# Fetching the second half's first operands one block later, and another order of statistics and copies in the opening

## The chip, the cores and the metric

The kernel runs on one core of a Trainium2 chip. The metric is device time in microseconds (us), the median of three runs. The core has five engines with instruction queues of their own, each worked through in order: TensorE (PE; its weight loads are shown as PEld), VectorE (DVE), ScalarE (ACT), GpSimd (POOL) and SyncE (SP). SP computes nothing here. It issues nearly all DMA transfers, and a transfer that has to wait for something holds up all transfers behind it in SP's queue. Tiles lie in SBUF, matmul results in PSUM banks.

## The reference

All values are float32. x has 2048 rows of 1024 features, there are 32 heads of 32 features, and the hidden width of the gated part is 3584.

```python
xn = layernorm(x)
# A: linear attention with learned softmax features
q, k, v = split(xn @ wqkv)                     # 32 heads of 32
pq, pk = q @ w_phi, k @ w_phi                  # per head
phi_q = concat(softmax(pq), softmax(-pq))
phi_k = concat(softmax(pk), softmax(-pk))
num = phi_q @ (phi_k^T @ v)
den = phi_q @ sum_s(phi_k) + 1e-6
s = (num / den) @ wo
# B: gated feed-forward
out = (silu(xn @ w1) * (xn @ w3)) @ w2
result = x + s * silu(out)
```

## The kernel before

Every float32 operand is split in two parts, a high one (a cast to a 32-bit matmul type, on ACT) and the low rest (a subtraction, on DVE). `split` (L92) does both, so L95 is the cast and L96 the subtraction. A product takes three passes (`PASSES`, L90). The large products are multiplied two by two in blocks with seven products instead of eight. The seven are listed in `ORDER`: each names a PSUM bank (a, b or c) and its two operands, A11, A12, S2, S1, S3, S4, A22 from the rows and B11, B21, T2, T1, T3, B22, T4 from the weights.

The first large stage is gate and up (x @ w1, x @ w3). It goes over the rows in two halves, tb 0 and 1. In each half it goes over 28 feature blocks f, and in each block over the seven products j. One such product is a step: 12 matmuls of 128x512 on TensorE (L655). The list `events` holds all steps in order. `gate_up(step)` issues a step's matmuls and whatever else is tied to it, and returns `read`, which reads the bank: copies and activations on ACT, additions and products on DVE.

The instructions of this stage are recorded in the order in which the code writes them (`in_order`, engine by engine). No scheduler moves them. What is tied to which step is set by tables:

- `load_at`: when the weights of a later block are fetched (`b_load`, `b_part`, L265, two transfers of 512 KB into one of two buffers named rw).
- `sums_at`: when the sums of the weight blocks are made (`b_sums`, L131 and L132).
- `prep_at`: when the next of the seven weight operands is split (`b_operands`).
- `before` and `after`: side work that rides along, such as `side_kv` (prepares the weights for the keys and values from tiles of the pool "xp", and stores the splits as wkv_d, L454) and `side_fold`.

`gate_up` also fetches the row operands of the second half. The operands of the first half lie in seven large slots. Two more slots belong to the pool "spare", which is opened only when the pools "xp" and "bdp" are closed, and lies in their place. A transfer into "spare" therefore waits until the last reader of "xp" is done. The first two operands of the second half (A11 and A12, named op1A, four transfers each, `fetch`, L167) go there. The other five follow from the last block on, each when a slot comes free. In the last block of the second half the same lines fetch weights for the next stage.

```python
if f == NF - 3 and j == 0:
    if tb == 0:
        close("xp", "bdp")
        spare = pool("spare", 1, side="right")
    for m in range(2):
        early.update(fetch(tb + 1, m))
```

Ahead of step 4 stands the opening, written out by hand. It loads eight tiles of 128 rows. The first four are normalised and turned (transposed on TensorE, L223), and steps 0 to 3 are computed from them. The other four (late_x) follow: `stats` (mean and variance, L196 and L197), `rstd` (the root on ACT, L203, then a refinement on DVE, L207 to L212), `norm` (L218), the turns, copies out of PSUM (`raw_x`, L228), sums and splits. Between them stand the folds: 12 blocks of the key weights are multiplied with w_phi on TensorE (`first_folds`, L252), copied back by ACT and stored (`first_copies`, L343 and L344), and the next ones are loaded (`load_folds`, L245). Turns and folds share three PSUM banks. `next(gens[0, f])` splits the next weight operand of block f; those in question are the two T2 operands, which step 4 and step 5 need.

Of the kernel before, what the change touches and what calls it, by code (L numbers as in the profile page):

```python
# [20 lines left out]
NF = FF // P  # L21
# [8 lines left out]
def tile_kernel(ctx: ExitStack, tc: tile.TileContext, x, wkT, wqT, wv, wphi, wo, w1, w3, w2, out):  # L30
# [3 lines left out]
    def pool(name, bufs, **kw):  # L34

        open_pools[name] = tc.tile_pool(name=name, bufs=bufs, reuse_waits="tile", **kw)
        return open_pools[name].__enter__()

    def close(*names):
        for name in names:  # L40
            open_pools.pop(name).__exit__(None, None, None)
# [51 lines left out]
    def split(hi, lo, src, by=None):  # L93

        nc.scalar.copy(hi, src)  # L95
        (by or nc.vector).tensor_sub(lo, src, hi.bitcast(F))  # L96
# [58 lines left out]
    def slot(m, j):  # L155
        name = f"op{m}" + (ANAMES if m < 2 else BNAMES)[j]
        j = HOMES[m][j]
        if j < 7:
            return big.tile([P, 2, 4, 512], R, name=name, tag=f"big{j}")
        return spare.tile([P, 2, 4, 512], R, name=name, tag=f"spare{j}")  # L160

    def fetch(m, j):
        t = slot(m, j)
        if m < 2:
            n = ANAMES[j]
            for q in range(4):
                nc.sync.dma_start(t[:, :, :, q * P:(q + 1) * P].bitcast(F), xo_d[m][n][:, q])  # L167
        else:
            n = BNAMES[j]
            nc.sync.dma_start(t.bitcast(F), wkv_d[(1, 2, 0)[m - 2]][n])  # L170
        return {n: t}
# [7 lines left out]
    def flat(t):  # L179
        return t.rearrange("p k t -> p (k t)")  # L180
# [12 lines left out]
    def stats(mv, j, xt):  # L193
        st = small.tile([P, 2, 6], F, name="st")
        for a in range(2):
            nc.vector.bn_stats(st[:, a, :], xt[a])  # L196
        nc.vector.bn_aggr(mv[:, j], st.rearrange("p a b -> p (a b)"))  # L197
# [50 lines left out]
    def fold(wr, c):  # L248

        pw = ps.tile([P, 4, P], F, name="pw", tag="tr", bufs=3)  # L250
        for g in range(4):
            nc.tensor.matmul(pw[:, g, :], wr[:, g], bd[:, 4 * c + g, :], start=True, stop=True)  # L252
        return pw
# [3 lines left out]
    def b_load(f):  # L257

        rw = rwp.tile([P, 2, 2, 512], F, name="rw", tag="rw")
        for a in range(2):  # L260
            b_part(rw, f, a)
        return [rw[:, a, h] for a in range(2) for h in range(2)]
# [25 lines left out]
    ao, xs = {n: slot(0, j) for j, n in enumerate(ANAMES) if n in ("A11", "A12", "S2", "S1")}, []  # L288
# [38 lines left out]
    def first_split(n, qs=range(4)):  # L327
        for q in qs:
            sl = slice(q * P, (q + 1) * P)
            split(ao[n][:, 0, :, sl], ao[n][:, 1, :, sl], raw[q][n])  # L330

    def first_folds(n):
        for _ in range(n):
            k = first_folds.at
            assert k not in to_load
            to_copy.append((k, fold(fold_rooms[k % 6], folds[k][2])))
            first_folds.at += 1

    def first_copies(n):
        for _ in range(n):  # L340
            k, pw = to_copy.pop(0)
            wr = fold_rooms[k % 6]
            nc.scalar.copy(wr, pw)  # L343
            nc.sync.dma_start(folds[k][3], flat(wr))  # L344
# [23 lines left out]
    mvs = [consts[:, 8 + 8 * k:16 + 8 * k].rearrange("p (j a) -> p j a", a=2) for k in range(2)]  # L368
# [15 lines left out]
    def blk2(k):  # L384
        if not rooms:
            rooms.extend(big.tile([P, 8, 512], F, name="room", tag=f"big{j}") for j in (2, 3))
        return rooms[k // 8][:, k % 8]
# [214 lines left out]
    for u in range(2 * NKB):  # L602
        f = 4 * (u // 2) + 2 * (u % 2)
# [20 lines left out]
    xo, early, gens, bos, silus = {}, {}, {}, {}, []  # L624
# [3 lines left out]
    def gate_up(step):  # L628
        nonlocal spare
        tb, f, j = events[step]  # L630
        last = f == NF - 1
        b, an, bn = ORDER[j]
        if f == NF - 3 and j == 0:
            if tb == 0:
                close("xp", "bdp")
                spare = pool("spare", 1, side="right")
            for m in range(2):
                early.update(fetch(tb + 1, m))
        for late in load_at.get(step, ()):
            rws.append(b_load(late[1]))  # L640
        for do in before.pop(step, ()):
            do()
        bank = banks.setdefault((tb, f), {})

        paired = (tb, f) == (1, 1)
        first = b not in bank
        if first:
            if paired and b == "a":
                bank[b] = ps.tile([P, 512], F, name="banka", tag="tr", bufs=3)
            else:  # L650
                bank[b] = ps.tile([P, 512], F, name=f"bank{b}", bufs=BANKS[b])
        n = 0
        for k in range(4):
            for u, w in PASSES:
                nc.tensor.matmul(bank[b], bos[tb, f][bn][:, w, k], ao[an][:, u, k], start=first and n == 0,  # L655
                                 stop=LAST[b] == an and n == 11, skip_group_check=True)
                n += 1
        for g in prep_at.get(step, ()):
            next(gens[g])
        for g in sums_at.get(step, ()):  # L660
            bos[g] = {}
            gens[g] = b_operands(rws.pop(0), bos[g])
            next(gens[g])
        for do in after.pop(step, ()):
            do()

        def read():

            nonlocal ao, early, hs, even, even_d, bank
            def part(name):  # L670
                if paired:
                    t = blk2(10 + len(part_names))
                    part_names.append(name)
                else:
                    t = flat(blk(name)) if (tb, f) == (0, 1) else work.tile([P, 512], F, name=name, tag="w")
                parts[tb, f, name] = t
                return t

            h0, u0, u1 = (parts.get((tb, f, name)) for name in ("h0", "u0", "u1"))
            hd = h_d[tb][f // 4][:, :, :, f % 2, f % 4 // 2]  # L680
            if an == "A11":
                nc.scalar.copy(part("h0"), bank["b"])
            elif an == "A12":
                nc.vector.tensor_add(h0, bank["a"], h0)
                if step < 4:
                    silus.append(h0)
                else:
                    nc.scalar.activation(h0, h0, AF.Silu)
            elif an == "S2":
                nc.scalar.copy(part("u0"), bank["b"])  # L690

                for d, b, t in hs:
                    store_h(d, b, t)
                hs = []
            elif an == "S1":
                nc.scalar.copy(part("u1"), bank["c"])
            elif an == "S3":
                nc.vector.tensor_add(u1, bank["b"], u1)  # L698
            elif an == "S4":
                nc.vector.tensor_add(u0, bank["c"], u0)  # L700
                nc.vector.tensor_mul(h0, h0, u0)
                hs.append((hd, 0, h0))
            else:
                h1 = work.tile([P, 512], F, name="h1", bufs=2)
                nc.scalar.activation(h1, bank["b"], AF.Silu)
                nc.vector.tensor_mul(h1, h1, u1)
                if f % 2 == 0:
                    even, even_d = h1, hd
                else:
                    nc.vector.tensor_add(even, even, h1)  # L710
                    hs += [(even_d, 1, even), (hd, 1, h1)]
                for name in ("h0", "u0", "u1"):
                    del parts[tb, f, name]
                del banks[tb, f], bos[tb, f], bank
                h0 = u0 = u1 = h1 = None
            if last and tb:
                xo.update(reload(0, [ANAMES[0], ANAMES[1]] if j == 0 else ANAMES[j + 1:j + 2]))
            if last and j < 5:
                early.update(fetch(tb + 1, j + 2))
            if last and j == 6:  # L720
                ao, early = early, {}

        return read
# [20 lines left out]
    def early_raw(t, h):  # L744
        raw[t][early_at(t, h)[0]] = raw_x(pts.pop((t, h)))
# [25 lines left out]
    reads[0]()  # L771
    for t in range(4):
        early_raw(t, 1)
    next(gens[0, 1])
    reads[1]()
    reads.append(gate_up(2))
    first_folds(2)
    first_copies(2)
    stats(mvs[1], 0, xs[4])
    stats(mvs[1], 1, xs[5])  # L780
    reads[2]()
    reads.append(gate_up(3))
    first_folds(4)
    load_folds(2)
    first_copies(2)

    nc.gpsimd.tensor_copy(consts[:, 1:2], mvs[1][:, 0, 0:1])
    for do in held:
# [3 lines left out]
        stats(mvs[1], t, xs[4 + t])  # L792
    r1 = rstd(mvs[1], sds[1])
    next(r1)
    first_copies(2)
    load_folds(2)
    sd = next(r1)
    for t in range(4):
# [11 lines left out]
    first_sums("S1", (2, 3))  # L810
    first_sums("S2", (2, 3))
    first_split("S2", (2, 3))
    first_folds(2)
    first_copies(2)
    for f in range(2):
        next(gens[0, f])
    first_folds(1)
    first_copies(2)
    assert first_folds.at == FOLDS and not to_copy
# [706 lines left out]
```

## Time and profile before

| what | value |
|---|---|
| runs (us) | 2388.48, 2393.23, 2399.55; median 2393.23 |
| profiled execution, its own time | 2389.33 us |
| its span, first to last instruction | 2387.5 us |
| TensorE busy | 2347.3 us, 98% |
| VectorE busy | 1774.7 us, 74% |
| ScalarE busy | 898.5 us, 38% |
| GpSimd busy | 257.4 us, 11% |
| mean granted TensorE clock | 0.995 |

A row of a timeline reads: start (us from the span's start), length in us, engine, line, operation, output<-input, shape, count, and in brackets the idle time before it with what ended it. Rows of one kind that follow one another on an engine are merged, so the length can span several. SPq is SP's queue issuing a transfer. A row of a waits view reads: engine, what it was about to do, what it waited for, total us, number of times, longest. A row of a windows view gives a stretch, its length, and then the busy time (with the count of instructions) of PE, PEld, DVE, ACT and POOL, the granted clock, the DMA share and the GB/s.

### The profile page before, as it was taken

What the parts mean: (1) busy time and instruction counts of PE and PEld (TensorE: products, weight loads), DVE (VectorE), ACT (ScalarE), POOL (GpSimd) and SP (SyncE); (2) the same over time, 40 slices, a digit from 0 to 9 for tenths busy, and PEclk for the clock granted to TensorE, in tenths of its full rate; (3) what the DMA queues carried; (4) which work ended last, traced back from release to release, by engine and by line L of the source; (5) the groups of instructions that cost most, each with busy time, mean ns of one, the idle gap of its engine ahead of it and who ended that gap; (6) DMA issues with size and microseconds to landing.
All of it is one profiled execution on the core that took longest, in us unless ns stands there. A gap on an engine that the chain in (4) does not pass through costs nothing.

```text
span 2387.5 us, 37640 instructions
## 1 busy us (share of the span) xinstructions
PE 2347.3 (98%) x14592; PEld 1924.1 (81%) x14592; DVE 1774.7 (74%) x2777; ACT 898.5 (38%) x1577; POOL 257.4 (11%) x243
## 2 busy tenths in 40 slices
PE   7999999997999999999999999999999999999999
PEld 6888888886888888888788888887888888888787
DVE  7877778884688888875466665777577888786775
ACT  5545444443355544543212221334433333353000
POOL 1000000000000000000000000331012222213562
PEclk9999999998999999999999999999999999999999
DMA  5446689995988898954977878997435653479763
GB/s 214 146 163 216 225 280 309 322 306 191 310 289 277 301 301 286 302 200 169 400 285 258 318 256 292 366 332 256 154 126 158 203 177 132 150 246 274 206 185 103
DMA packets 298354, 578.03 MB, mean 242 GB/s; under 512 B 24624, under 2 KB 151744, under 8 KB 295488
## 3 DMA queue, kind: packets, MB, share of 16 engines
q1 hardware_dynamic: 291840, 552.56, 68.8%
q10 hardware_dynamic: 6336, 23.07, 2.4%
q8 instruction: 115, 1.88, 0.3%
q14 instruction: 63, 0.52, 0.1%
HBM read 372.64 MB, written 202.91 MB: 241 GB/s over the span
## 4 chain that ended last, share of the span: by engine, by line
PE 94%; DVE 2%; DMA 2%; SPq 1%; ACT 0%; issue 0%; POOL 0%; DVEq 0%; ACTq 0%; POOLq 0%
PE bankb L655 25%; PE bankb L1280 13%; PE bankc L655 12%; PE pm L1432 8%; PE bankb L875 7%; PE bankc L1280 6%; PE banka L655 6%; PE bankb L942 4%; PE bankc L875 3%; PE banka L1280 3%; PE bankc L942 2%; PE banka L875 2%; PE po L1417 1%; PE banka L942 1%; PE pkv L860 1%; DMA op2T<-wkv_d1T 1%
## 5 line engine op out<-in xcount | busy, mean ns | idle before, releaser
L96 DVE TENSOR_TENSOR bo<-rw,bo 128x512 fp32r<-128x512 f32 x336 | 230.8, 688 | 153.6 <-ACT bo L95 153.2
L1280 PE MATMUL bankb<-bo,as 128*128 128x512 f32 x960 | 235.2, 389 | 1.3 <-ACT acc L1286 1.3
L95 ACT CAST bo<-rw 128x512 fp32r<-128x512 f32 x336 | 206.7, 618 | 17.6 <-DMA w_d2B<-w2o 3.1
L1280 PEld LDWEIGHTS bankb<-bo,as 128*128 128x128 f32 x960 | 180.1, 188 | 39.1 <-ACT acc L1286 1.7
L655 PE MATMUL bankb<-op0S,bo 128*128 128x512 f32 x672 | 166.5, 398 | 14.8 <-ACT u L690 14.0
L655 PE MATMUL bankc<-op0S,bo 128*128 128x512 f32 x672 | 163.6, 392 | 0.3 <-DVE op0S L96 0.3
L655 PEld LDWEIGHTS bankb<-op0S,bo 128*128 128x128 f32 x672 | 128.4, 192 | 42.8 <-ACT u L690 14.4
L655 PE MATMUL bankb<-op1S,bo 128*128 128x512 f32 x672 | 161.2, 389 | 0.0
L655 PE MATMUL bankc<-op1S,bo 128*128 128x512 f32 x672 | 161.2, 389 | 0.0
L1432 PE MATMUL pm<-wos,oT 128*128 128x512 f32 x672 | 160.0, 393 | 0.0
L655 PE MATMUL bankb<-op0A,bo 128*128 128x512 f32 x672 | 159.2, 391 | 0.7 <-ACT op0A L738 0.7
L852 POOL MEMSET ev<- 128x32 f32 x32 | 4.2, 132 | 1435.6 <-DVE bo L96 1100.0
L1280 PE MATMUL bankc<-bo,as 128*128 128x512 f32 x624 | 158.4, 389 | 0.0
L655 PE MATMUL bankb<-op1A,bo 128*128 128x512 f32 x672 | 157.6, 390 | 0.0
L655 PEld LDWEIGHTS bankc<-op0S,bo 128*128 128x128 f32 x672 | 125.4, 188 | 30.1 <-issue 2.9
L655 PEld LDWEIGHTS bankb<-op1A,bo 128*128 128x128 f32 x672 | 125.9, 188 | 27.4 <-DVE u L698 1.3
L655 PEld LDWEIGHTS bankb<-op0A,bo 128*128 128x128 f32 x672 | 125.2, 188 | 27.9 <-ACT op0A L738 0.9
L655 PEld LDWEIGHTS bankc<-op1S,bo 128*128 128x128 f32 x672 | 126.1, 188 | 26.2
L655 PEld LDWEIGHTS bankb<-op1S,bo 128*128 128x128 f32 x672 | 126.1, 188 | 26.2
L1432 PEld LDWEIGHTS pm<-wos,oT 128*128 128x128 f32 x672 | 124.8, 188 | 27.5 <-DVE oT L1423 0.3
L1280 PEld LDWEIGHTS bankc<-bo,as 128*128 128x128 f32 x624 | 117.1, 188 | 24.4
L1294 DVE TENSOR_TENSOR acc<-bankb,acc 128x512 f32<-128x512 f32 x152 | 102.0, 685 | 31.2 <-PE bankb L1280 31.2
(272 smaller groups left out, 4332.4 us busy)
## 6 DMA issues: line engine op xcount, KB each, us to landing
rw<-in_w SPq DMA_DIRECT2D x112, 512.0 KB, 4.5
hr<-h_d SPq DMA_DIRECT2D x56, 512.0 KB, 4.7
h_d<-h SPq DMA_DIRECT2D x111, 256.0 KB, 5.2
xoS<-xo_d0S SPq DMA_DIRECT2D x44, 512.0 KB, 6.3
xoS<-xo_d1S SPq DMA_DIRECT2D x44, 512.0 KB, 5.9
xoA<-xo_d0A SPq DMA_DIRECT2D x33, 512.0 KB, 4.9
xoA<-xo_d1A SPq DMA_DIRECT2D x33, 512.0 KB, 5.1
e_d<-eq ACTq DMA_DIRECT2D x32, 512.0 KB, 6.1
```

Of the source, the lines that this page charges most:

```text
L95: nc.scalar.copy(hi, src)
L96: (by or nc.vector).tensor_sub(lo, src, hi.bitcast(F))
L655: nc.tensor.matmul(bank[b], bos[tb, f][bn][:, w, k], ao[an][:, u, k], start=first and n == 0, stop=LAST[b] == an and n == 11, skip_group_c ...
L852: nc.gpsimd.memset(v[:, :, DH:], 1.0)
L860: nc.tensor.matmul(pkv[sl, m], e[:, m // 4, (m % 4) * P + 32 * h:(m % 4) * P + 32 * h + 32], v[:, 4 * (m % 4) + h], start=first and m == 0 ...
L875: nc.tensor.matmul(bank[b], xo[an][:, u, k], wb[bn][:, w, k], start=an in ("A11", "A12", "S1") and n == 0, stop=LAST[b] == an and n == 11, ...
L942: nc.tensor.matmul(bank[b], xo[an][:, u, k], wb[bn][:, w, k], start=an in ("A11", "A12", "S1") and n == 0, stop=LAST[b] == an and n == 11, ...
L1280: nc.tensor.matmul(bank[b], t[:, u, pos + k], bos[kb, bn, k][:, w], start=first and n == 0, stop=LAST[b] == an and n == 5, skip_group_chec ...
L1294: nc.vector.tensor_add(c, pb, c)
L1417: nc.tensor.matmul(po[32 * j:32 * j + 32, a, 64 * k:64 * k + 64], kvs[sl, j, c, k], et[sl, :, 4 * k + j], start=True, stop=True, skip_grou ...
L1432: nc.tensor.matmul(p, oTs[t, h][:, a, k], wos[c, 4 * h + k][:, b], start=n == 0, stop=n == 3 * ND - 1)
```

## The change

Three places are edited.

- In `gate_up` the close of "xp" and "bdp", the opening of "spare" and the fetch of the second half's first two operands happen at block 26 (NF - 2) of the first half instead of block 25. In the second half the place stays at block 25.
- In the opening the statistics of late tile 4 stand ahead of the second split of block 1's weights instead of behind the first fold copies. Two fold copies that stood ahead of the statistics' root now stand behind it.
- At the end of the opening the split of block 0's T2 stands ahead of two folds and two fold copies, and the split of block 1's T2 stays behind them.

```diff
@@ gate_up
-        if f == NF - 3 and j == 0:
+        if f == NF - (3 if tb else 2) and j == 0:
             if tb == 0:
                 close("xp", "bdp")
                 spare = pool("spare", 1, side="right")
@@ opening
     for t in range(4):
         early_raw(t, 1)
+    stats(mvs[1], 0, xs[4])
     next(gens[0, 1])
     reads[1]()
     reads.append(gate_up(2))
     first_folds(2)
     first_copies(2)
-    stats(mvs[1], 0, xs[4])
     stats(mvs[1], 1, xs[5])
     reads[2]()
     reads.append(gate_up(3))
     first_folds(4)
     load_folds(2)
-    first_copies(2)
 ...
     r1 = rstd(mvs[1], sds[1])
     next(r1)
-    first_copies(2)
+    first_copies(4)
     load_folds(2)
     sd = next(r1)
 ...
     first_split("S2", (2, 3))
+    next(gens[0, 0])
     first_folds(2)
     first_copies(2)
-    for f in range(2):
-        next(gens[0, f])
+    next(gens[0, 1])
     first_folds(1)
     first_copies(2)
```

What stands on SP's queue around the fetch (L167), before. L454 stores splits of `side_kv`, L613 stores h, L265 fetches a block's weights; the first L265 row is block 26's, the second block 27's:

```order
L265 DMA rw<-in_w 128x1024 x2
L454 DMA wkv_d2T_119<-wkvo 256x1x512
L454 DMA wkv_d2B_120<-wkvo 256x1x512
L454 DMA wkv_d2T_121<-wkvo 256x1x512
L167 DMA op1A_4982<-xo_d1A_94 128x8x128 x4
L167 DMA op1A_4987<-xo_d1A_95 128x8x128 x4
L454 DMA wkv_d2B_115<-wkvo 256x1x512
L454 DMA wkv_d2B_116<-wkvo 256x1x512
L613 DMA h_d_6_63<-h_4839 128x4x128
L265 DMA rw<-in_w 128x1024 x2
L454 DMA wkv_d2T_117<-wkvo 256x1x512
```

The same place on SP after the change, from block 27's weights on:

```order
L613 DMA h_d_6_63<-h_4839 128x4x128
L265 DMA rw<-in_w 128x1024 x2
L454 DMA wkv_d2T_117<-wkvo 256x1x512
L454 DMA wkv_d2T_118<-wkvo 256x1x512
L454 DMA wkv_d2T_119<-wkvo 256x1x512
L454 DMA wkv_d2B_120<-wkvo 256x1x512
L167 DMA op1A_5139<-xo_d1A_94 128x8x128 x4
L167 DMA op1A_5144<-xo_d1A_95 128x8x128 x4
L454 DMA wkv_d2T_121<-wkvo 256x1x512
L613 DMA h_d_6_63<-h_4998 128x4x128
L613 DMA h_d_6_63<-h_4974 128x4x128
L613 DMA h_d_6_63<-h_5130 128x4x128
```

The eight fetches moved from ahead of block 27's weights to behind them; the last split's store, three stores of h and the weights of the second half's block 0 follow them.

On ACT in the opening, around the root of the second statistics (L203; room_b and wr are the rooms of the folds, pw a fold's bank):

```order
 L95 CAST bo<-rw 128x512
-L682 COPY h_472<-bankb 128x512
-L343 COPY room_b<-pw 128x512 x4
+L682 COPY h_476<-bankb 128x512
+L343 COPY room_b<-pw 128x512 x2
 L203 ACTIVATE consts<-consts 128x4
+L343 COPY room_b<-pw 128x512 x2
 L343 COPY wr<-pw 128x512 x2
```

Two of four fold copies moved from ahead of the root to behind it.

On ACT some rows later, at the end of the opening (t_345 and t_386 are the T2 of block 0 and block 1, op0S_264 is the operand S2):

```order
 L343 COPY room_b<-pw 128x512 x2
 L95 CAST op0S_264<-room_a 128x4x128 x2
+L95 CAST bo<-t_345 128x512
 L343 COPY room_b<-pw 128x512 x2
-L95 CAST bo<-t_345 128x512
 L95 CAST bo<-t_386 128x512
 L343 COPY wr<-pw 128x512 x2
```

The cast of block 0's T2 moved ahead of two fold copies. On TensorE and GpSimd the order of the instructions is unchanged, and on VectorE only the statistics of late tile 4 changed places with one split of a weight operand.

## The prediction

> **What bounds the kernel now.** The page first: its head, its chain, and the sizes of the transfers that matter below (KB each, median us from issue to landing).
>
> ```profile
> span 2387.5 us, 37640 instructions
> ...
> PE 94%; DVE 2%; DMA 2%; SPq 1%; ACT 0%; issue 0%; POOL 0%; DVEq 0%; ACTq 0%; POOLq 0%
> ...
> rw<-in_w SPq DMA_DIRECT2D x112, 512.0 KB, 4.5
> ...
> h_d<-h SPq DMA_DIRECT2D x111, 256.0 KB, 5.2
> ...
> wkv_d2T<-wkvo SPq DMA_DIRECT2D x16, 512.0 KB, 8.4
> ...
> op1A<-xo_d1A SPq DMA_DIRECT2D x12, 512.0 KB, 6.4
> ```
>
> TensorE carries 94% of the chain, so only what stops it is worth time. Its waits, longest first, begin with
>
> ```profile
> PE bankb L655 <- ACT u L690: 14.0, 1, 14.0
> ```
>
> One wait, 14.0 us, once. TensorE in order of time around it:
>
> ```profile
> 563.51 2.88 PE L655 MATMUL bankc<-op0S,bo 128*128 128x512 f32 x12
> 580.41 5.49 PE L655 MATMUL bankb<-op0S,bo 128*128 128x512 f32 x12 [14.03 <-ACT u L690]
> 585.70 3.21 PE L655 MATMUL bankc<-op0S,bo 128*128 128x512 f32 x12
> 588.75 5.60 PE L655 MATMUL bankb<-op0A,bo 128*128 128x512 f32 x24
> ...
> 610.51 2.88 PE L655 MATMUL bankb<-op1A,bo 128*128 128x512 f32 x12
> ```
>
> From 588.75 to the turn (the first product with op1A, 610.51) lie eight steps of 12 matmuls, 2.72 us each. At that pace the step at 588.75, three after 563.51, would have begun at 571.67. So this place costs 588.75 - 571.67 = 17.08 us: 14.03 idle, and 3.05 because the first steps behind the gap run slowly. The clock in these stretches (last three numbers: granted clock, DMA share, GB/s):
>
> ```profile
> 554.25:588.75 34.50, 20.47 (x78) 16.34 (x77) 11.28 (x17) 7.09 (x13) 0.00 (x0) 0.75 0.97 320
> ...
> 580.41:588.75 8.34, 8.34 (x24) 6.62 (x25) 4.16 (x7) 2.57 (x5) 0.00 (x0) 0.65 0.80 286
> ```
>
> ACT is named as releaser, so I followed the wait back, with all engines in order of time:
>
> ```profile
> 553.53 0.69 DVE L96 TENSOR_TENSOR wkvo<-wkv,wkvo 128x512 fp32r<-128x512 f32 x1 [1.79 <-ACT wkvo L95]
> ...
> 561.64 0.69 DVE L96 TENSOR_TENSOR bo<-rw,bo 128x512 fp32r<-128x512 f32 x1 [1.99 <-ACT bo L95]
> ...
> 576.69 0.69 DVE L131 TENSOR_TENSOR rw<-rw 128x512 f32<-128x512 f32 x1 [14.35 <-DMA rw<-in_w]
> 578.02 0.68 DVE L684 TENSOR_TENSOR h<-banka,h 128x512 f32<-128x512 f32 x1
> 579.78 0.58 ACT L690 COPY u<-bankb 128x512 f32<-128x512 f32 x1
> ...
> 596.74 0.68 DVE L131 TENSOR_TENSOR rw<-rw 128x512 f32<-128x512 f32 x1
> ```
>
> VectorE is free at 562.33 and stands 14.35 us before the sums of block 27's weights, because the weights are not there. Behind the sums it reads bank a (578.02), ACT then copies bank b (579.78), and TensorE gets the bank at 580.41: 3.72 us from weights to TensorE. Why the weights are late is told by the SP queue's waits and then by its order of time:
>
> ```profile
> SPq L167 <- DVE wkvo L96: 24.3, 1, 24.3
> ```
>
> ```profile
> 526.48 0.82 SPq L265 DMA_DIRECT2D rw<-in_w  x2
> ...
> 529.33 0.57 SPq L454 DMA_DIRECT2D wkv_d2T<-wkvo  x1
> 554.25 10.67 SPq L167 DMA_DIRECT2D op1A<-xo_d1A  x8
> 564.97 2.49 SPq L454 DMA_DIRECT2D wkv_d2B<-wkvo  x2
> ...
> 568.17 1.88 SPq L265 DMA_DIRECT2D rw<-in_w  x2
> ```
>
> The first of the eight fetches (L167) stands 24.3 us until the last split from the pool "xp" ends at 553.53 + 0.69 = 554.22, since its destination lies where that pool was. Block 27's weights (L265), three stores behind it, are issued at 568.17 and are there at 576.69.
>
> **The change, part one: the fetch.** On SP the eight fetches go back past block 27's weights, six wkv stores and one of h. Nothing is added.
>
> - The fetch still needs the end of the split at 554.22, and the store just ahead of it needs a split that is older. It starts at 554.25 as before. Its own wait shrinks, and block 27's weights are no longer behind it. One block (7 x 2.72 = 19.04 us) after the pair at 526.48 they go out at 545.5. At the 8.5 us that the late pair took to be used they are there at 554.0, and they are wanted at 562.33. The stall goes: -17.08 us.
> - What is late next? Without the gap the sums stand at 562.33 + 3.72 = 566.05 from TensorE, which wants the bank at 563.51 + 2.72 = 566.23. It fits by 0.18 us, so I allow 0 to 0.5 us there.
> - Behind the fetch now stand one store, three h_d and the weights of the second half's block 0. They are wanted at 596.74 - 17.08 = 579.66. Bytes from 554.25 on: 8 x 512 + 512 + 3 x 256 + 2 x 512 = 6400 KB, 6.55 MB; at the 320 GB/s of the row above 20.5 us, so there by 574.7. Other end: the old spacing, 568.17 - 554.25 = 13.9 us to the issue, one store more ahead of it (+1.2 us, half of the 2.49 at 564.97), and 8.5 us to use: 577.9. Both are in time; margin 1.8 to 5.0 us.
> - The turn wants op1A at 610.51 - 17.08 = 593.4. Issues end at 564.97, plus 6.4 us: 571.4. Cover 22 us.
>
> [...]
>
> The 3.05 us beside the idle 14.03 is clock, 0.65 granted. [...]
>
> **Part two: the opening.** It is bound by a chain over all engines until about 70 us.
>
> ```profile
> 26.12 0.69 DVE L96 TENSOR_TENSOR bo<-rw,bo 128x512 fp32r<-128x512 f32 x1 [1.95 <-ACT bo L95]
> 26.73 1.28 DVE L196 BATCH_NORM_STATS2 st<-late_x 128x6 f32<-128x512 f32 x2
> ...
> 32.82 0.21 DVE L197 BATCH_NORM_AGGREGATE consts<-st 128x2 f32<-128x12 f32 x1
> 35.98 0.18 DVE L207 RECIPROCAL consts<-consts 128x4 f32<-128x4 f32 x1 [2.96 <-ACT consts L203]
> ```
>
> ```profile
> 34.28 0.58 ACT L343 COPY room_b<-pw 128x512 f32<-128x512 f32 x1 [4.04 <-PE pw L252]
> ...
> 35.65 0.30 ACT L203 ACTIVATE consts<-consts 128x4 f32<-128x4 f32 x1
> 36.96 0.58 ACT L343 COPY wr<-pw 128x512 f32<-128x512 f32 x1 [0.31 <-PE pw L252]
> 38.35 0.59 ACT L228 COPY room_a<-pt 128x512 f32<-128x512 f32 x1 [0.81 <-PE pt L223]
> ...
> 43.16 1.22 ACT L95 CAST op0S<-room_a 128x512 fp32r<-128x512 f32 x2 [0.80 <-DVE room_a L360]
> ...
> 48.08 1.06 ACT L343 COPY room_b<-pw 128x512 f32<-128x512 f32 x2
> 49.03 1.15 ACT L95 CAST bo<-t 128x512 fp32r<-128x512 f32 x2
> ```
>
> ```profile
> 30.35 3.00 PE L655 MATMUL banka<-op0A,bo 128*128 128x512 f32 x12 [0.73 <-ACT room_b L343]
> ...
> 37.69 3.92 PE L223 MATMUL pt<-ident,late_x 128*128 128x128 f32 x32 [0.77 <-DVE late_x L218]
> ```
>
> - Tile 4's statistics (1.28 + 0.21 us) move into VectorE's 1.95 us of idle time before 26.12. All four end about 1.4 us sooner, 33.03 to 31.6.
> - The root (0.30 us) was at 35.65 behind two fold copies that waited for TensorE. Ahead of them it runs in ACT's 4.04 us of idle time, at 31.6; VectorE goes on at about 32.0 instead of 35.98, 4.0 us earlier.
> - Late next: TensorE and ACT. The 0.73 us at 30.35 ends with VectorE's addition from bank a, which moves up too, and the 0.77 us at 37.69 goes: the turns start about 1.5 us sooner. ACT's first raw copy then follows the fold copy of 36.96 directly, which itself moves up 0.7 to 0.8: 0.8 + 0.81 = 1.6 us sooner. Its casts at 43.16 lose their 0.80 us as well, for VectorE is done with the norms early: 2.4 us.
> - At 48.08 the T2 cast now goes ahead of two fold copies. The cast comes 0.95 us sooner, but the last fold on TensorE waits one cast (0.57 us) longer for its bank, and the first S2 product is behind that fold. Between -0.5 and +0.4 us; I take +0.2, since VectorE carries the stretch behind it, 24.83 us busy (the third number with its count) in 25:
>
> ```profile
> 50.00:75.00 25.00, 23.94 (x96) 18.84 (x96) 24.83 (x42) 19.29 (x36) 0.00 (x0) 0.93 0.32 112
> ```
>
>
> Sum 2.6 us. Low end: TensorE's own two waits alone less the cast, 0.73 + 0.77 - 0.57 = 0.9. High end: the root's 4.0. The moved stores of folds go with their copies; the loads behind them on SP keep their order.
>
> **Sum.** 17.1 + 2.6 = 19.7 us off. The profiled execution took 2389.33 us (2387.5 of span): 2369.6. The median of the runs, 2393.23, is 3.9 us above it, which would give 2373.5. I take 2371, between.
>
> **Rivals.**
> - *A second wait behind the fetch.* Block 0's weights of the second half come after 579.66 because four megabytes are ahead of them. For it: it is the very mechanism of the stall now, and the margin by one reckoning is 1.8 us. Against it: fewer bytes compete than now, 6.55 MB against 320 GB/s x 34.5 us = 11.0 MB. Price one for one beyond 579.66, some 4 to 10 us: 2375 to 2381.
> - *The change doesn't lift the stall.* Block 27's weights are held by something else in the queue, such as the wkv stores now directly ahead of them, or by their buffer. For it: the block's sums are at most 0.18 us from TensorE. Against it: at 526.48 the same queue issued the block before with the same kind of stores ahead. Only the opening is left: about 2389.
> - *Slower: the fetch is too late for the turn.* TensorE stands at the first product with op1A if that lands after 593.4, one for one, and beyond 593.4 + 19.7 = 613.1 the kernel is slower than before. For it: the fetch is placed one block closer to its use and still starts only when the pool is free. Against it: 571.4 as reckoned. A fetch that lands 45 us later than reckoned, at 616.4, would give 2392 + 3.9 for the median's place, 2396. [...]
>
> **Chances.** Forecast 0.78 (2364 to 2377), second wait 0.11, no lift 0.08, slower 0.03. About 0.5% (12 us: below 2381.3 is faster) is what a measurement of this kernel can tell from no change. Faster: the forecast and half of the second wait, with a little off for the runs' own spread (2388.48 to 2399.55), 0.83. Same: no lift and the rest, 0.13. Slower 0.04. The range reaches from 2363 (opening at its high end, against the profiled time, less spread) to 2382, which takes in the second wait.
>
> **What would show it.** In the changed profile TensorE's wait on ACT's L690 is gone and 12-matmul steps run at 2.72 us from 500 to 640; VectorE's sums of block 27 have no DMA wait; the SP wait at L167 is under 5 us; the clock stays at 1.00 there. In the opening the root stands at about 31.6 and the turns start at about 36.2. I am wrong if a wait on rw<-in_w appears again one block later, or if TensorE stands at the first op1A product.

## The result, and the profile after

The changed kernel takes 2371.92 us (median of 6 runs, 2369.19 to 2373.16) against 2391.82 for the kernel before on the same occasions. The ratio is 0.9914, with a 95% interval from 0.9897 to 0.9931: 0.86% faster, about 20 us. 2371 was forecast. The profiled execution took 2372.7 us.

The page of the changed kernel, its head and its chain:

```profile
span 2370.9 us, 37641 instructions
...
PE 93%; DVE 3%; DMA 2%; ACT 1%; issue 0%; POOL 0%; SPq 0%; DVEq 0%; ACTq 0%; POOLq 0%
```

TensorE's waits in the changed kernel, the longest first:

```profile
PE banka L750 <- DMA xt<-in_x: 7.1, 1, 7.1
PE pt L223 <- DVE xt L218: 2.2, 1, 2.2
PE pw L252 <- ACT room_b L343: 1.9, 1, 1.9
...
PE bankb L655 <- ACT u L690: 0.9, 1, 0.9
```

The 14.0 us at L655 are gone. What is left of that name is 0.9 us at another place (below). TensorE in order of time around block 26 and the turn:

```profile
561.68 2.88 PE L655 MATMUL bankc<-op0S,bo 128*128 128x512 f32 x12
564.40 2.88 PE L655 MATMUL bankb<-op0S,bo 128*128 128x512 f32 x12
567.12 2.88 PE L655 MATMUL bankc<-op0S,bo 128*128 128x512 f32 x12
569.85 5.60 PE L655 MATMUL bankb<-op0A,bo 128*128 128x512 f32 x24
...
591.61 2.88 PE L655 MATMUL bankb<-op1A,bo 128*128 128x512 f32 x12
```

Steps of 2.72 us without a gap, and the turn at 591.61 instead of 610.51. The SP queue there:

```profile
543.70 0.81 SPq L265 DMA_DIRECT2D rw<-in_w  x2
...
550.55 13.42 SPq L167 DMA_DIRECT2D op1A<-xo_d1A  x8
...
568.28 1.36 SPq L265 DMA_DIRECT2D rw<-in_w  x2
575.48 10.32 SPq L167 DMA_DIRECT2D op1S<-xo_d1S  x8
```

Block 27's weights go out at 543.70, ahead of the fetch. VectorE's sums of three successive blocks:

```profile
558.19 0.69 DVE L131 TENSOR_TENSOR rw<-rw 128x512 f32<-128x512 f32 x1
...
577.83 0.69 DVE L131 TENSOR_TENSOR rw<-rw 128x512 f32<-128x512 f32 x1
...
593.77 0.69 DVE L131 TENSOR_TENSOR rw<-rw 128x512 f32<-128x512 f32 x1 [2.66 <-DMA rw<-in_w]
```

The first two, block 27 and block 0 of the second half, don't wait. The third, block 1, waits 2.66 us (1.34 in the kernel before); TensorE's step at 597.04 then takes 2.76 us instead of 2.72.

In the opening, from the timelines of all engines:

```profile
27.32 1.60 DVE L96 TENSOR_TENSOR bo<-rw,bo 128x512 fp32r<-128x512 f32 x1 [0.51 <-ACT bo L95]
...
33.78 0.30 ACT L203 ACTIVATE consts<-consts 128x4 f32<-128x4 f32 x1 [2.34 <-DVE consts L197]
...
37.48 3.94 PE L223 MATMUL pt<-ident,late_x 128*128 128x128 f32 x32
...
68.24 5.28 PE L655 MATMUL bankc<-op0S,bo 128*128 128x512 f32 x22 [0.29 <-DVE op0S L96]
```

The root and the turns come sooner than before (35.65 and 37.69), though this execution's second step began 1.2 us later than before's (23.30 against 22.10). To take that out, I cut each profile at three points that TensorE's timeline shows in every kernel: the start of the second step (the first product that follows the second group of turns), the opening's last product (bank c with the low part of S4), and the turn (first op1A product). All in us:

| kernel | second step at | to the last product of the opening | on to the turn | on to the end | span |
|---|---|---|---|---|---|
| before | 22.10 | 47.91 | 540.50 | 1776.99 | 2387.5 |
| changed | 23.30 | 44.94 | 523.37 | 1779.29 | 2370.9 |
| changed, again | 21.10 | 44.93 | 523.39 | 1777.98 | 2367.4 |
| fetch alone | 21.10 | 47.89 | 523.35 | 1776.96 | 2369.3 |
| opening alone | 24.44 | 45.46 | 540.18 | 1776.42 | 2386.5 |
| ahead of the weights | 23.22 | 44.89 | 533.44 | 1779.85 | 2381.4 |
| behind the weights | 24.56 | 45.51 | 523.30 | 1777.73 | 2371.1 |
| last block | 22.19 | 45.61 | 523.35 | 1781.85 | 2373.0 |
| w2 sums later | 21.00 | 44.93 | 523.32 | 1778.85 | 2368.1 |
| root only | 22.06 | 45.62 | 523.29 | 1779.73 | 2370.7 |
| swap only | 21.05 | 47.81 | 523.37 | 1778.67 | 2370.9 |
| GpSimd later | 22.24 | 44.38 | 523.44 | 1778.14 | 2368.2 |

The column up to the last product of the opening belongs to the opening, the one up to the turn to the fetch. The start of the second step and the stretch to the end move on their own: 23.30 and 21.10, 1779.29 and 1777.98 in the two profiles of the changed kernel.

### The profile page after: what moved, and what is told of

Its sections match the earlier page's. It is cut to its first block, busy times and chain, and to the rows that moved or that the text cites. A ratio compares the mean times of both kernels' runs of the same rounds, so it can differ in the third digit from the quotient of the medians.

```text
span 2370.9 us, 37641 instructions
## 1 busy us (share of the span) xinstructions
PE 2345.3 (99%) x14592; PEld 1922.2 (81%) x14592; DVE 1774.7 (75%) x2777; ACT 897.9 (38%) x1577; POOL 257.6 (11%) x243
## 4 chain that ended last, share of the span: by engine, by line
PE 93%; DVE 3%; DMA 2%; ACT 1%; issue 0%; POOL 0%; SPq 0%; DVEq 0%; ACTq 0%; POOLq 0%
PE bankb L655 24%; PE bankb L1279 13%; PE bankc L655 12%; PE pm L1431 8%; PE bankb L874 7%; PE bankc L1279 6%; PE banka L655 6%; PE bankc L874 3%; PE banka L1279 3%; PE bankb L941 3%; PE banka L874 2%; PE bankc L941 1%; PE po L1416 1%; PE pkv L859 1%; DMA xoA<-xo_d0A 1%; PE banka L941 1%
## 5 line engine op out<-in xcount | busy, mean ns | idle before, releaser
L96 DVE TENSOR_TENSOR bo<-rw,bo 128x512 fp32r<-128x512 f32 x336 | 231.6, 691 | 151.6 <-ACT bo L95 151.3
L655 PE MATMUL bankc<-op0S,bo 128*128 128x512 f32 x672 | 163.2, 392 | 0.3 <-DVE op0S L96 0.3
L655 PE MATMUL bankb<-op0S,bo 128*128 128x512 f32 x672 | 162.1, 390 | 1.3 <-ACT op0S L95 0.6
L655 PE MATMUL bankb<-op1S,bo 128*128 128x512 f32 x672 | 161.4, 389 | 0.9 <-ACT u L690 0.9
L655 PE MATMUL bankc<-op1S,bo 128*128 128x512 f32 x672 | 161.5, 389 | 0.1
L655 PE MATMUL bankb<-op0A,bo 128*128 128x512 f32 x672 | 160.6, 394 | 0.7 <-ACT op0A L738 0.7
L655 PE MATMUL bankb<-op1A,bo 128*128 128x512 f32 x672 | 157.7, 390 | 0.0
L655 PEld LDWEIGHTS bankb<-op0A,bo 128*128 128x128 f32 x672 | 126.5, 190 | 28.2 <-ACT op0A L738 1.1
L655 PEld LDWEIGHTS bankc<-op0S,bo 128*128 128x128 f32 x672 | 125.0, 188 | 29.9 <-issue 2.5
L655 PEld LDWEIGHTS bankb<-op0S,bo 128*128 128x128 f32 x672 | 125.6, 188 | 28.0 <-DVE op0S L96 1.1
L655 PEld LDWEIGHTS bankb<-op1S,bo 128*128 128x128 f32 x672 | 126.0, 188 | 27.5 <-ACT u L690 1.3
L655 PEld LDWEIGHTS bankb<-op1A,bo 128*128 128x128 f32 x672 | 125.8, 188 | 27.5 <-DVE u L698 1.3
L655 PEld LDWEIGHTS bankc<-op1S,bo 128*128 128x128 f32 x672 | 126.0, 188 | 26.6 <-DVE bo L96 0.5
```

## The experiments

Theory: SP works in order (in the profile of before the fetch stands 24.3 us, and block 27's weights, behind it in the queue, go out at 568.17), so having them behind the waiting fetch is what stopped TensorE, and the opening is a separate gain of 2 to 3 us. The first rivals: the parts depend on each other, the distance of the move is what counts, or the stores behind the fetch matter too.

**The fetch alone.** The kernel before with one line changed:

```diff
-        if f == NF - 3 and j == 0:
+        if f == NF - (3 if tb else 2) and j == 0:
```

> The kernel before with the fetch alone moved to block 26; the opening as before. Theory (the two parts add up): the wait of 14.0 us at L655 on ACT's u is gone as in the changed kernel, and the time is 14 to 16 us under before, about 2376.5, some 2 us above the changed kernel's times less what the opening's first microseconds vary by. Rival (the opening's gain is what the profile of the changed kernel shows by chance, or the fetch's gain depends on the opening): the time is the changed kernel's own, 2372, or well above 2380.

Measured: 2375.27 us, 0.994 of before (0.9924 to 0.9957). The opening is before's to 0.02 us (47.89) and the stretch to the turn is 523.35, 17.15 shorter. No wait of TensorE is left between 400 and 800 us.

**The opening alone.** The changed kernel with that line as before.

> The changed opening alone, the fetch at block 25 as before. Theory: the last product of the opening (bank c with S4) starts 1.8 to 2.6 us sooner than the 70.01 us of before, the wait of 14 us stays, and the time is 1 to 3 us under before: 0.999. Rival (the opening gives nothing that lasts): within 0.5 us of before, since an earlier start only lengthens the wait at block 26.

Measured: 0.9995 of before (0.9985 to 1.0004), 2388.31 against 2389.97 us. By the times the opening alone can't be told from no change; the interval allows 3.6 us off to 1.0 us on. By the profile it is 2.45 us shorter from the second step on (45.46 against 47.91), and nothing of that is lost up to the turn (540.18 against 540.50). The start of the second step took it back in this execution, 24.44 against 22.10, ahead of anything that the change touches. The long wait stands as it was, by TensorE's waits:

```profile
PE bankb L655 <- ACT u L690: 13.8, 1, 13.8
```

Both profiles have the same granted clock in the opening (0.89 between 45 and 60 us, below). By these stretches the two parts add up, and most of the result is the fetch's; the intervals of the times are too wide to show that they add up.

**How far must the fetch move?** Two kernels, one step apart, with the changed opening:

```diff
-        if f == NF - (3 if tb else 2) and j == 0:
+        if f == NF - 3 and j == (0 if tb else 3):   # the other one: else 4
```

At step 3 the fetch is still just ahead of block 27's weights on SP, at step 4 just behind them.

> The changed kernel with the fetch at block 25, step 3 of the block: three steps later than before, and still just ahead of block 27's weights on SP's queue. Theory (what counts is whether these weights stand behind the waiting fetch): TensorE's wait of about 14 us is back almost whole, 11 to 14 us, and the time is 2386 to 2390. Rival (a fetch that is issued later waits less, whatever stands behind it): three of the seven steps give back about three sevenths of the 17 us, and the time is about 2381.

> The changed kernel with the fetch at block 25, step 4: one step later than in the run with step 3, and just behind block 27's weights on SP's queue. Theory (the weights behind the waiting fetch are the whole of it): no wait above 1 us at L655 on ACT's u, 2371 to 2374 as the changed kernel. Rival (the stores of the side work's splits, which still stand behind the waiting fetch, hold buffers that the casts on ACT need): TensorE waits 2 to 8 us around block 26, 2375 to 2381.

Measured: 2380.81 us (0.9966, 0.9953 to 0.9979) ahead of the weights, 2371.81 us (0.9924, 0.991 to 0.9939) behind them. One step later is worth the 10.1 us between 533.44 and 523.30 in the table, and behind the weights everything is regained: the move by a whole block gives no more than this move by four steps. The SP queue and TensorE with the fetch ahead:

```profile
537.65 0.61 SPq L613 DMA_DIRECT2D h_d<-h  x1
550.41 10.20 SPq L167 DMA_DIRECT2D op1A<-xo_d1A  x8
560.66 2.15 SPq L265 DMA_DIRECT2D rw<-in_w  x2
```

```profile
561.54 2.88 PE L655 MATMUL bankc<-op0S,bo 128*128 128x512 f32 x12
571.72 5.46 PE L655 MATMUL bankb<-op0S,bo 128*128 128x512 f32 x12 [7.30 <-ACT u L690]
```

and with the fetch behind:

```profile
545.46 0.81 SPq L265 DMA_DIRECT2D rw<-in_w  x2
...
552.31 10.54 SPq L167 DMA_DIRECT2D op1A<-xo_d1A  x8
562.89 2.11 SPq L454 DMA_DIRECT2D wkv_d2T<-wkvo  x2
```

With the fetch behind the weights, SP still stands 5.4 us at L167 with stores behind it, and TensorE's wait on u is 0.3 us. The rival that such stores stop ACT's casts, and TensorE with them, falls for a wait of this length. In the kernel with the fetch ahead my number was wrong. I expected 11 to 14 us of idle time, and it is 7.3 (and another 0.9 behind the turn). Three stores now go ahead of the fetch instead of between it and the weights, so the weights follow it directly: from the start of the fetch to their issue it is 560.66 - 550.41 = 10.25 us instead of 568.17 - 554.25 = 13.92, 3.7 less. And the fetch itself starts 1.9 us sooner, counted from the opening's last product (550.41 - 68.11 = 482.30, before 554.25 - 70.01 = 484.24). VectorE then takes the weights up sooner after their issue:

```profile
568.00 0.69 DVE L131 TENSOR_TENSOR rw<-rw 128x512 f32<-128x512 f32 x1 [9.87 <-DMA rw<-in_w]
```

That is 568.00 - 560.66 = 7.34 us instead of 576.69 - 568.17 = 8.52, 1.2 less. From TensorE's restart to the turn it takes 601.55 - 571.72 = 29.83 us instead of 610.51 - 580.41 = 30.10, 0.3 less. Together this is the whole 7.1 us by which 533.44 is shorter than 540.50. The rival "later waits less" gave the right total by chance, three sevenths of the gain; it gives no jump from step 3 to step 4.

**One block later still.** The other-side rival of the prediction, the fetch too late for the turn, pushed one block further: the line reads `NF - (3 if tb else 1)`.

> The changed kernel with the fetch at the first half's last block, 27, one block later still. Theory (the turn has some 20 us of cover, so a later fetch costs nothing at the first op1A product; it only crowds the transfers of the turn): SP issues it from about 563, it has landed by about 582, the turn wants it at about 592, no wait there; the weights of the second half's block 1 come 0 to 2 us later than in the changed kernel, where VectorE stood 2.66 us for them. 2372 to 2376. Rival (the fetch becomes exposed, or the transfers of the turn pile up into a new wait): TensorE waits 5 us or more between 590 and 620, 2377 to 2385.

Measured: 2374.74 us, 0.9941 (0.992 to 0.9962). SP issues the fetch from 562.55, and the first op1A product doesn't wait. The stretch to the turn is 523.35 once more. What suffers lies behind the turn, on VectorE and then in TensorE's waits:

```profile
594.84 0.69 DVE L131 TENSOR_TENSOR rw<-rw 128x512 f32<-128x512 f32 x1 [4.19 <-DMA rw<-in_w]
...
621.73 0.69 DVE L131 TENSOR_TENSOR room<-room 128x512 f32<-128x512 f32 x1 [5.74 <-DMA room<-in_w]
```

```profile
PE bankb L655 <- DVE bo L96: 1.3, 1, 1.3
PE bankb L655 <- ACT u L690: 0.9, 1, 0.9
PE bankc L655 <- DVE bo L96: 0.7, 1, 0.7
```

2.9 us of waits from transfers that crowd together. The theory holds at the turn, and the rival's second half (a pile-up of transfers) is there, smaller than the 5 us it was given.

**What is given back behind the turn.** In the changed kernel TensorE waits 0.9 us at about 626, behind the first sums of w2's weights. VectorE stood 5.11 us for those, 3.19 in the kernel before. I planned these sums two steps later in the changed kernel:

```diff
-        at_ = room(s0 + 4, 2 * OP_US)
+        at_ = room(s0 + (6 if u == 0 else 4), 2 * OP_US)
```

> The changed kernel with the sums of the first w2 unit of the second half planned two steps later (the later units' places follow from it). Theory (behind the turn TensorE gives back 1.3 us at about 624 to 627 because VectorE stands 5.11 us before these sums, whose weights come late behind the turn's transfers): the 0.9 us wait at L655 on ACT's u between 600 and 700 is gone and the time from the turn to the end is 1 to 1.5 us shorter than the changed kernel's 1779.3 us, thus 2370.5. Rival (that wait is the transfers' variation from run to run, and the later place costs elsewhere): the same time or more, 2372 and up.

Measured: 2371.43 us, 0.9925 (0.991 to 0.994), the changed kernel's own time. The 0.9 us wait is gone, but there is one of 1.1 us on VectorE's L96 at 596.18, behind block 1's weights, for which VectorE stood 4.02 us in this execution. It lies ahead of the moved sums. From the turn to the end it takes 1778.85, no shorter than the 1777.98 that the changed kernel shows in its second profile. So the aimed-at wait went, as the theory said (though the fetch alone shows none there either), but the shorter time that it promised didn't come. With one profile of this kernel a gain of 1 us can't be told from what the last stretch moves by on its own. In seven profiles the fetch is behind the weights and not at the last block, counting both of the changed kernel but not this one; the last stretch takes 1776.96 to 1779.73 there, and 1776.42 and 1776.99 with the fetch at block 25, step 0. Some 1 to 2 us are given back, then, on most occasions; the fetch alone gives back none (1776.96 against 1776.99). That the late transfers are the cause is argued from their waits, not shown.

**The parts of the opening.** Two kernels, with the fetch moved in both, one execution each:

```diff
 # root only: the changed opening with the end as before
-    next(gens[0, 0])
     first_folds(2)
     first_copies(2)
-    next(gens[0, 1])
+    for f in range(2):
+        next(gens[0, f])
 # swap only: the opening of before with these lines the other way round
```

> The changed kernel with the T2 split of block 0 back behind the two folds and copies, so that of the opening only the statistics and the root are moved. From the second step's start to the S4 product with the low part the kernel before takes 47.9 us and the changed one 44.9. Theory (the root is worth 2.4, the swap of the T2 cast 0.2): 45.1 to 45.5. Rival (the swap is worth a good part): 46 and more.

> The kernel before with the fetch moved and, of the opening, only the T2 split of block 0 ahead of the two folds and copies. Theory (the swap is worth 0.2, between -0.5 and +0.4): 47.5 to 48.4 us from the second step's start to the S4 product with the low part, against 47.9 before. Rival: under 47.

Measured: 45.62 us with the root only, 47.81 with the swap only, 47.91 before (spans 2370.7 and 2370.9). Taken as they stand, the root and the statistics give 2.3 us and the swap 0.1. But the changed opening as a whole has been 44.9 (four profiles) or 45.5 to 45.6 (three), and what tells these apart is TensorE's granted clock between 45 and 60 us (the third number from the end). In the kernel before, with the opening alone, in the changed kernel, and with the root only:

```profile
45.00:60.00 15.00, 13.04 (x60) 10.76 (x61) 13.98 (x24) 12.77 (x24) 0.00 (x0) 0.89 0.28 107
```

```profile
45.00:60.00 15.00, 12.85 (x63) 10.91 (x63) 14.12 (x24) 12.91 (x24) 0.00 (x0) 0.89 0.28 107
```

```profile
45.00:60.00 15.00, 13.12 (x68) 10.89 (x66) 14.61 (x25) 14.12 (x26) 0.00 (x0) 1.00 0.26 97
```

```profile
45.00:60.00 15.00, 12.47 (x56) 9.87 (x56) 13.97 (x24) 14.36 (x27) 0.00 (x0) 1.00 0.21 76
```

It is 1.00 in all four of the short ones and 0.89 in all three of the long ones; in the first the opening's first 24 products with S2 take 5.7 us, in the others 6.6 to 7.2. The kernel before, the fetch alone and the swap only have 0.89, the root only has 1.00. At 0.89, then, the whole change of the opening is worth 2.3 to 2.5 us (45.46 to 45.61 against 47.89 and 47.91) and the swap alone 0.1. At 1.00 the swap is worth 0.7 on top of the root, by the one profile of the root only (44.9 against 45.62); there TensorE's wait for ACT ahead of the next S2 products is longer with the root only (first line) than in the changed kernel (second line):

```profile
60.27 0.73 PE L655 MATMUL bankb<-op0S,bo 128*128 128x512 f32 x2 [1.21 <-ACT op0S L95]
```

```profile
60.84 0.73 PE L655 MATMUL bankb<-op0S,bo 128*128 128x512 f32 x2 [0.64 <-ACT op0S L95]
```

What the root is worth by itself stays open, since its profile and the one of before have different clocks. Whether the new order makes the higher clock more likely stays open too: the openings with the old root had 0.89 in all three profiles.

**Why VectorE's split takes 1.60 us.** In the changed kernel's opening one split at L96 takes 1.60 us instead of 0.69. At the same time GpSimd makes the sums for T2 (the first from 27.09, the split from 27.32), which begin when late tile 4's mean is there, and that mean is now made sooner. I let them wait for tile 5's mean:

```diff
-    nc.gpsimd.tensor_copy(consts[:, 1:2], mvs[1][:, 0, 0:1])
+    nc.gpsimd.tensor_copy(consts[:, 1:2], mvs[1][:, 1, 0:1])
```

> The changed kernel with GpSimd's four sums for the T2 operands held until the statistics of late tile 5 instead of tile 4 (the small copy ahead of them reads tile 5's mean). Theory (VectorE's split of block 1's weights, which took 0.69 us before and takes 1.60 in the changed opening, is stretched by GpSimd's sums that now run beside it): the split is back at 0.69, the first of the sums at about 29 us does no harm there, and the opening from the second step to the S4 product with the low part is 0.2 to 0.9 us shorter than the changed kernel's 44.9 to 45.6. The time hardly tells, 2371 to 2372. Rival (the split is long for its own reason, its input or its place): 1.60 us again.

Measured: 2370.96 us, 0.9914 (0.99 to 0.9929). VectorE and GpSimd in this kernel:

```profile
26.25 0.69 DVE L96 TENSOR_TENSOR bo<-rw,bo 128x512 fp32r<-128x512 f32 x1 [0.51 <-ACT bo L95]
...
32.81 1.13 DVE L211 TENSOR_SCALAR consts<-consts 128x4 f32<-128x4 f32 x1
```

```profile
28.66 1.28 POOL L131 TENSOR_TENSOR rw<-rw 128x512 f32<-128x512 f32 x1
```

The split is back at 0.69, and the opening is 44.38, 0.55 shorter than the changed kernel's 44.93, with the granted clock at 1.00 between 45 and 60 us in both. A part of the gain goes again: the refinement's L211, 0.17 us in the changed kernel, now runs beside GpSimd's sums and takes 1.13. It is the fastest opening of all the profiles. In the whole time its 0.5 us can't be told from the changed kernel beside it.

**The changed kernel once more**, on the same chip as that run:

> The changed kernel once more beside it, on the same chip. Theory (the opening's length from the second step on is one of two values by the granted clock at 50 to 58 us, and the second step's own start varies with the clock of the first 20 us, whatever the kernel): second step between 21.0 and 24.6, from there 44.9 or 45.5, the stretch to the turn 523.3 to 523.4, 2370 to 2374 in all. Rival (these are properties of the built kernel): 23.3 and 44.94 again to 0.1.

Measured: 2371.47 us, 0.9922 (0.9905 to 0.9938). The second step starts at 21.10 instead of 23.30, the opening is 44.93, the stretch to the turn 523.39. The start is no property of the kernel. The opening's length came out the same, as did its granted clock, 1.00.

## Why the prediction was right

Point by point, by its own steps:

- **The fetch, -17.08 us.** Measured 540.50 - 523.37 = 17.13. The 3.05 us of slow clock came back with the idle time: the granted clock from 554.25 to 588.75 is 1.00 in the changed kernel, where it was 0.75.
- **Block 27's weights out at 545.5.** 543.70, which on before's clock (its opening ended 1.77 us later) is 545.5. They were wanted at 558.19, and VectorE didn't wait.
- **"It starts at 554.25 as before."** Not quite. On before's clock the fetch starts at 552.3, because its own wait ends 1.9 us sooner. In the kernel before, the cast for the last split waits for TensorE:

```profile
552.88 0.62 ACT L95 CAST wkvo<-wkv 128x512 fp32r<-128x512 f32 x1 [2.10 <-PE bankc L655]
```

In the changed kernel it stands at 547.61 without a wait. A possible cause is that the stores stuck behind the fetch hold buffers of the pool that the casts write to. It fits that the wait of 2.10 us is there with the opening alone too, and that it is gone at steps 3 and 4, where three of these stores go ahead of the fetch; but the profile names TensorE as the releaser, and no run tests it.
- **The second half's block 0 in time.** Yes: issued at 568.28, no wait at 577.83. The eight issues took 13.42 us instead of 10.67.
- **Op1A in time, cover 22 us.** Yes, and the run with the last block spent more than half of that cover without a wait at the turn.
- **0 to 0.5 us left at block 26.** 0. The sums of block 27 began at 558.19, on before's clock 560.0 and not 562.33, so that the margin was some 2.5 us instead of 0.18.
- **The opening, -2.6 us.** 2.97 in this pair of profiles, 2.3 to 3.0 over all of them, but some 0.5 of the 2.97 goes with the granted clock between 45 and 60 us, 1.00 against 0.89; at the same clock it is 2.3 to 2.5. The terms are less sure than their sum. The swap, +0.2 expected, was worth 0.1 without the root at 0.89 and 0.7 with it at 1.00, above the +0.4 that was allowed; it was priced as a term of its own, and its worth seems to hang on how early TensorE is there. And 0.55 us were lost to GpSimd, which the prediction left out: it counted the order on GpSimd as unchanged and didn't ask when its work would start. The root came at 33.78, on before's clock (1.20 us) 32.6 and not 31.6; 0.9 of that is the split of 1.60 us.
- **Not in the sum:** the microseconds given back behind the turn, and the start of the second step, 21.0 to 24.6 us over the profiles. They are as large as the opening's whole gain. That the median came within 1 us of 2371 is therefore in part luck; that the fetch's term came out to 0.1 us is not.
- **The place between profile and median.** I took 2371 between 2369.6 and 2373.5. The kernel before has since given medians of 2389.97 to 2391.82, so the first median was on the high side.
- **The rivals.** "No lift" and "too late" did not come. A second wait behind the fetch did come in small, one block later than I had placed it.

## What to carry to other kernels

On an in-order queue look at what stands behind a transfer that waits, and not only at when the transfer is needed. Here four steps of code order, just enough to let one pair of loads go first, were worth 17 us; and a prefetch that couldn't start yet was better issued behind the loads that could and were wanted sooner. Put off by one block more it crowded the next loads. When work is pulled forward, follow every engine that its result releases, the ones with an unchanged order too. And cut profiles at fixed points before comparing spans, and compare the granted clock of each stretch as well: the stretch to the turn came out the same to 0.15 us in nine profiles, where whole runs differ by five, while the opening's length moved by 0.5 us with its clock (44.9 at 1.00, 45.5 at 0.89).

## What the runs showed of the hardware

Two things that I had not expected.

The start of the second step moves by up to 3.6 us, ahead of anything that was changed. Most of it arises on TensorE's first step and on the turns just ahead of it. In the kernel before, in the kernel with the opening alone, and in the changed kernel's second profile:

```profile
17.30 3.29 PE L655 MATMUL bankb<-op0A,bo 128*128 128x512 f32 x12 [0.68 <-ACT op0A L738]
```

```profile
17.58 5.36 PE L655 MATMUL bankb<-op0A,bo 128*128 128x512 f32 x12 [0.68 <-ACT op0A L738]
```

```profile
15.95 0.73 PE L655 MATMUL bankb<-op0A,bo 128*128 128x512 f32 x2 [0.78 <-ACT op0A L738]
17.00 2.60 PE L655 MATMUL bankb<-op0A,bo 128*128 128x512 f32 x10 [0.32 <-DVE op0A L742]
```

The same twelve matmuls take 3.3 or 5.4 us behind the same short idle time in the first two. In the third the first step begins 1.35 us sooner than in the first; the 16 turns ahead of it begin at 13.2 in all three, and there they take 2.02 us instead of 3.47. The clock column shows 1.00 from 12 to 22 us in all three, so it doesn't tell them apart. In the changed kernel's first profile, where the first step takes 4.64 us, it shows 0.66 there. What sets these lengths, no run here shows.

VectorE and GpSimd were both slower side by side here. A subtraction of two SBUF tiles on VectorE (L96) took 1.60 us instead of 0.69 while GpSimd added such tiles, one of GpSimd's sums (L132) took 1.60 instead of 1.28, and both were back, at 0.69 and 1.29, when GpSimd began later. The small L211 of 128x4, which reads one tile only, went from 0.17 to 1.13 us beside GpSimd. Why, no run here shows.
